# Two-layer attention kernel: the main loop's order on the four compute engines written out by hand, and the first v loads spread over chunks

## The chip, the cores and the metric

The kernel runs on one core of one Trainium2 chip. The metric is device time of one execution in microseconds. It was run three times before the change: 2247.88, 2250.13 and 2253.04 us, median 2250.13 us.

## The reference

For each of two batches, q and k (6080 x 256) are normalised per column, S = kn^T qn / tau is a 256 x 256 matrix, a softmax runs over its last axis, and v (6080 x 256) is multiplied with it. The result x (12160 x 256) goes through two layers with a hidden width of 2048:

```python
h = x @ w_in;  r = np.maximum(h, 0.0);  g = s * (r * r) + b;  x = g @ w_out     # layer 1
h = x @ w2_in; g = h * np.cos(h);       x = g @ w2_out                          # layer 2
```

q and k arrive as float32; the weights arrive as float64 and are turned into float32 on the chip.

## The kernel before

**Numbers.** Every float32 operand is split into a rounded part hi and a remainder lo (`split`, L84: a copy on ScalarE, a subtraction on VectorE or GpSimd), and a product takes three matmuls: hi*hi, hi*lo, lo*hi (`product`, L294).

**Stages.** A prologue (L494 to L578) computes S of batch 0 from 15 chunks of rows; a full chunk has four tiles of 128 rows, 24 matmuls. Chunk loads run three chunks ahead (`qk_load`, QB = 3). In chunk 8 (`c == last - 6`, L546) it also asks for the first two weight blocks (`cv_load`) and for the four v tiles of the first token pair (`x_load`, four DMAs of 64 KB each, in pieces of 128 bytes). Behind the chunks stand the conversion of the first two weight blocks (`cv_conv`), the turning of v (`x_turn`) and its splits, and the softmax (`soft_2`, `soft_3`). The softmax matrix is folded into w_in (`fold`), so that v itself is the input of layer 1.

**Main loop** (L762). The tokens are 12 pairs of two column blocks (512 columns, 480 in every sixth pair); the hidden width is 8 slices. A unit is one pair and one slice, 96 units for each layer, 192 in all. The eight units of the first pair are plain (`in_plain`: 48 matmuls with those of `out`). All later ones use a Winograd product of seven instead of eight block products: with its 24 output matmuls a unit has 21 + 24 = 45. A unit k runs its seven products in four groups, `in_1` and `in_5`, `in_62`, `in_73`, `in_4`, with the outputs of unit k-1 between them (`out`, in the order 0, 1, 3, 2); its element work is `el_a` (relu, or the whole turns of the cosine), `el_b` (square, or sine and product) and `el_c` (split), which straddle units k and k+1. In PSUM there are two banks "s" (`a` and `e` of a unit), one "u" and one "x" (`b` of a unit; "x" alone for side work in layer 1), and four for the outputs "y".

**Around it.** In the units j = 0 to 7 of a pair the next pair's input is made ready: `x_load`, `x_turn` (layer 1), then seven operands (`x_step`: a subtraction for four of them, a split for each). At the first unit of a pair `drain` takes the four finished output blocks of the last pair out of PSUM, to DRAM. Side work is hung on slots of units (`at`): conversion of layer 1's weights (`cv_next`) and their folding in the plain pair, 48 chunks of the batch 1 matrix (`qk1_a`, `qk1_b`) in units 9 to 39, softmax and folding of batch 1 (`soft1`, `fold1`) in units 39 to 48, conversion of layer 2's weights (`cv2_next`, 16 blocks) in units 50 to 93, loads of them (`l2_load`) from unit 89 on.

**What sets the order.** The program is a list, but the instructions' order on each engine is chosen by a planner at build time: it takes what its own cost model holds to be ready, by priority. Slots run at a raised priority (`PW` = 30, L843), drains at `PV` = 40 (L827). SyncE's queue issues all DMAs.

```python
for fn in slot.pop(4 * k_ + s, []):    # L844, under tc.high_priority(offset=PW)
```

Of the kernel before, what the change touches and what calls it, by code (L numbers as in the profile page):

```python
# [28 lines left out]
GB = 8  # L29
# [11 lines left out]
def fused_kernel(ctx: ExitStack, tc: tile.TileContext, q, k, v, tau, w_in, w_out, ms, mb, w2_in, w2_out, res):  # L41
# [49 lines left out]
    def conv(raw, cp, nx=2):  # L91
# [101 lines left out]
    def combine_plain(j):  # L193
# [42 lines left out]
    def x_load(p, t, m):  # L236
# [11 lines left out]
        B[p, m, t] = r  # L248

    def x_turn(p, t, m):  # L250
        if p < NP:
            n = width(p)
            u = st("vturn")
            dve.transpose(out=u[:, 0:n], in_=B.pop((p, m, t))[:, 0:n])
            B[p, m, t] = u

    def x_split(p, nm, src):
        n = width(p)
        if p > NP and nm in ("T3", "T4"):
            hi, lo = [lp[0].tile([P, BLK], F32R, tag="xp", name=f"x{h}", bufs=8) for h in "hl"]  # L260
        else:
            hi, lo = [wk.tile([P, BLK], F32R, tag="xo", name=f"x{h}", bufs=XO) for h in "hl"]
        split(src[:, 0:n], hi[:, 0:n], lo[:, 0:n])
        X[p, nm] = (hi, lo)

    def x_sub(p, a, b):
        n = width(p)
        t = st("xt")
        dve.tensor_tensor(out=t[:, 0:n], in0=a[:, 0:n], in1=b[:, 0:n], op=ALU.subtract)  # L269
        return t  # L270

    def x_step(p, i):

        if i == 0:
            x_split(p, "B11", B[p, 0, 0])
        elif i == 1:
            B[p, "T1"] = x_sub(p, B[p, 0, 1], B[p, 0, 0])
            x_split(p, "T1", B[p, "T1"])
        elif i == 2:
            x_split(p, "B21", B[p, 1, 0])  # L280
        elif i == 3:
            B[p, "T2"] = x_sub(p, B[p, 1, 1], B[p, "T1"])
            x_split(p, "T2", B[p, "T2"])
# [21 lines left out]
    def in_plain(k_, i):  # L305
        f, t = divmod(i, 2)
        nh[0] += 1
        h = sbank() if nh[0] % 3 else bank("u")
# [4 lines left out]
    def in_1(k_):  # L313
        n = at_unit(k_)[3]
        U[k_, "a"] = a = sbank()
        product(a, k_, *IDX[1], True, False)
        l2 = k_ >= NL
        b = bank("x" if l2 and k_ % 2 else "u")
        if NL <= k_ < NL + 2:
            product(b, k_, *IDX[1], True, False)  # L320
        U[k_, "b"] = b

    def in_5(k_):
# [3 lines left out]
    def seed_b(k_):  # L327
# [4 lines left out]
    def copy_5(k_):  # L332
        n = at_unit(k_)[3]
        s5 = wm.tile([P, BLK], F32, tag="s5", name="s5", bufs=1)
        act.copy(out=s5[:, 0:n], in_=U[k_, "e"][:, 0:n])
        U[k_, "s5"] = s5

    def in_62(k_):
        n = at_unit(k_)[3]
        product(U[k_, "b"], k_, *IDX[6], False, False)  # L340
        e = U[k_, "e"]
        dve.tensor_tensor(out=e[:, 0:n], in0=U[k_, "s5"][:, 0:n], in1=U[k_, "b"][:, 0:n], op=ALU.add)  # L342
        product(U[k_, "a"], k_, *IDX[2], False, True)
        U[k_, 0], U[k_, 1] = U.pop((k_, "a")), e

    def in_73(k_):
        n = at_unit(k_)[3]
        product(U[k_, "b"], k_, *IDX[7], False, False)
        product(U.pop((k_, "e")), k_, *IDX[3], False, True)
# [4 lines left out]
    def in_4(k_):  # L354
# [4 lines left out]
    def el_a(k_, i):  # L359
        p, j, l, n = at_unit(k_)  # L360
        h = U[k_, i]
        plain = p == 0
        if l == 0:
            if i == 3 and not plain:
                RR[k_, i] = h
                return
            r = wm.tile([P, BLK], F32, tag="r", name="r", bufs=RB)
            act.activation(out=r[:, 0:n], in_=h[:, 0:n], func=AF.Relu)  # L368
        else:
            q_ = lp[0].tile([P, BLK], I32, tag="n2", name="n2", bufs=2)  # L370
            r = wm.tile([P, BLK], F32, tag="r", name="r", bufs=RB)
            act.activation(out=q_[:, 0:n], in_=h[:, 0:n], func=AF.Copy, bias=0.25)  # L372
            dve.scalar_tensor_tensor(out=r[:, 0:n], in0=q_[:, 0:n], scalar=-1.0, in1=h[:, 0:n], op0=ALU.mult, op1=ALU.add)  # L373
        RR[k_, i] = r

    def el_b(k_, i):
        p, j, l, n = at_unit(k_)
        r, h = RR[k_, i], U.pop((k_, i))
        if l == 0:
            if r is h:  # L380
                dve.scalar_tensor_tensor(out=r[:, 0:n], in0=h[:, 0:n], scalar=0.0, in1=h[:, 0:n], op0=ALU.max, op1=ALU.mult)
            elif i == 2 or p == 0 and i != 1:
                act.activation(out=r[:, 0:n], in_=r[:, 0:n], func=AF.Square)
            else:
                dve.tensor_tensor(out=r[:, 0:n], in0=r[:, 0:n], in1=h[:, 0:n], op=ALU.mult)  # L385
        else:
            act.activation(out=r[:, 0:n], in_=r[:, 0:n], func=AF.Sin, bias=HALF_PI, scale=TWO_PI)  # L387
            dve.tensor_tensor(out=r[:, 0:n], in0=r[:, 0:n], in1=h[:, 0:n], op=ALU.mult)  # L388
# [491 lines left out]
```

## Time and profile before

| | |
|---|---|
| runs | 2247.88, 2250.13, 2253.04 us; median 2250.13 us |
| the profiled execution's own time | 2245.69 us |
| its span, first to last instruction | 2243.9 us |
| instructions | 28456 |
| mean granted TensorE clock | 0.986 |

The profile shows one execution. In its tables PE is TensorE's matmuls, PEld its weight loads, DVE is VectorE, ACT ScalarE, POOL GpSimd, SP SyncE with its DMA queue SPq. An engine's line in a timeline has the start in us, the duration, the line of the kernel, what it writes and reads, and in brackets how long the engine had been idle and who released it. Matmuls are pipelined: a matmul's row lasts 0.39 us, while the next one starts 0.23 us after it, so the distance between starts is the price of one.

### The profile page before, as it was taken

Reading aid. Unit: us, or ns where it says so; the run is one execution under the profiler, and the core shown is the slowest. Engines: PE = TensorE matmul, PEld = TensorE weight load, DVE = VectorE, ACT = ScalarE, POOL = GpSimd, SP = SyncE. Lnnn points to the kernel's source line nnn. Section 1 sums busy time; section 2 is a strip of 40 time slices with the busy share of each in tenths; the row PEclk is TensorE's granted clock in tenths of the full one; section 3 lists DMA queues with packets and bytes.
Section 4 is the critical chain, followed back from the end, with each engine's and each line's share of the span. In section 5 each row is a group of like instructions: output and inputs, shape, how many; then the busy total and the mean of one; then the engine's idle time right before and its main releaser. Section 6 shows DMA issues by size and latency. Waiting matters only on the chain.

```text
span 2243.9 us, 28456 instructions
## 1 busy us (share of the span) xinstructions
PE 2135.6 (95%) x9478; PEld 1733.6 (77%) x9478; DVE 1708.5 (76%) x2412; ACT 1566.6 (70%) x2829; POOL 862.6 (38%) x638
## 2 busy tenths in 40 slices
PE   7799999999989999999999999999999999999998
PEld 7687788787877777788887877777777777777786
DVE  7896777767667988866668688687787787886875
ACT  6686666666666766665657777777777777777775
POOL 0012444334243323322223454444444545444544
PEclk9799999999999999999999999999999999999999
DMA  8531121220213424111042011011011011010111
GB/s 249 143 118 43 34 75 52 57 74 17 66 47 91 131 85 127 36 38 37 21 163 102 9 30 38 1 38 33 6 38 27 11 38 24 15 38 10 23 20 18
DMA packets 255524, 124.81 MB, mean 56 GB/s; under 512 B 206736, under 2 KB 221840, under 8 KB 255376
## 3 DMA queue, kind: packets, MB, share of 16 engines
q1 hardware_dynamic: 255376, 122.99, 20.4%
q8 instruction: 74, 1.21, 0.2%
q14 instruction: 74, 0.61, 0.1%
HBM read 82.31 MB, written 40.63 MB: 55 GB/s over the span
## 4 chain that ended last, share of the span: by engine, by line
PE 46%; DVE 14%; ACT 8%; issue 3%; DMA 1%; DVEq 0%; SPq 0%; POOLq 0%; ACTq 0%; POOL 0%
PE ps_y L408 24%; PE ps_s L299 12%; PE ps_u L299 6%; PE ps_x L299 3%; DVE xt L269 2%; DVE r L388 2%; ACT n L372 2%; ACT gh L85 2%; DVE r L373 2%; ACT r L387 2%; DVE xl L86 2%; DVE gl L86 1%; DVE r L385 1%; DVE ps_s L342 1%; DVE Af L170 1%
## 5 line engine op out<-in xcount | busy, mean ns | idle before, releaser
L86 POOL TENSOR_TENSOR gl<-r,gh 128x512 fp32r<-128x512 f32 (+1 forms) x560 | 747.9, 1342 | 1091.4 <-ACT gh L85 943.9
L85 ACT CAST gh<-r 128x512 fp32r<-128x512 f32 (+1 forms) x680 | 418.3, 615 | 242.5 <-DVE r L385 162.4
L408 PE MATMUL ps_y<-gh,WOh 128*128 128x512 f32 (+1 forms) x1536 | 483.2, 392 | 1.6 <-DVE dr L422 1.2
L408 PE MATMUL ps_y<-gh,WOl 128*128 128x512 f32 (+1 forms) x1536 | 482.9, 391 | 0.0
L408 PE MATMUL ps_y<-gl,WOh 128*128 128x512 f32 (+1 forms) x1536 | 477.9, 389 | 0.4 <-POOL gl L86 0.4
L408 PEld LDWEIGHTS ps_y<-gh,WOh 128*128 128x128 f32 x1536 | 288.6, 189 | 65.3 <-DVE dr L429 2.2
L408 PEld LDWEIGHTS ps_y<-gh,WOl 128*128 128x128 f32 x1536 | 290.0, 189 | 59.5 <-issue 0.2
L408 PEld LDWEIGHTS ps_y<-gl,WOh 128*128 128x128 f32 x1536 | 288.9, 189 | 60.4 <-POOL gl L86 1.2
L387 ACT ACTIVATE r<-r 128x512 f32<-128x512 f32 (+1 forms) x384 | 239.9, 628 | 133.5 <-DVE r L373 133.4
L299 PE MATMUL ps_s<-xh,WIh 128*128 128x512 f32 (+1 forms) x780 | 310.7, 398 | 11.6 <-DVE r L388 8.9
L299 PE MATMUL ps_s<-xh,WIl 128*128 128x512 f32 (+1 forms) x780 | 305.8, 393 | 0.0
L299 PE MATMUL ps_s<-xl,WIh 128*128 128x512 f32 (+1 forms) x780 | 305.4, 391 | 0.0
L299 PE MATMUL ps_u<-xh,WIh 128*128 128x512 f32 (+1 forms) x429 | 173.9, 405 | 32.1 <-DVE ps_s L342 16.8
L299 PEld LDWEIGHTS ps_s<-xh,WIh 128*128 128x128 f32 x780 | 147.5, 189 | 59.3 <-DVE r L388 24.6
L368 ACT ACTIVATE r<-ps_s 128x512 f32<-128x512 f32 (+1 forms) x198 | 116.9, 591 | 92.2 <-PE ps_s L299 91.5
L299 PEld LDWEIGHTS ps_s<-xh,WIl 128*128 128x128 f32 x780 | 147.4, 189 | 31.8
L299 PEld LDWEIGHTS ps_s<-xl,WIh 128*128 128x128 f32 x780 | 147.7, 189 | 28.2
L299 PE MATMUL ps_u<-xl,WIh 128*128 128x512 f32 (+1 forms) x429 | 167.5, 390 | 0.0
L299 PE MATMUL ps_u<-xh,WIl 128*128 128x512 f32 (+1 forms) x429 | 167.3, 390 | 0.0
L373 DVE SCALAR_TENSOR_TENSOR r<-n,ps_s 128x512 f32<-128x512 int32 (+1 forms) x192 | 130.0, 677 | 46.2 <-ACT n L372 45.0
L388 DVE TENSOR_TENSOR r<-r,ps_s 128x512 f32<-128x512 f32 (+1 forms) x192 | 129.4, 674 | 44.4 <-ACT r L387 42.5
L86 DVE TENSOR_TENSOR gl<-d,gh 128x512 fp32r<-128x512 f32 (+1 forms) x88 | 106.2, 1206 | 62.7 <-ACT gh L85 53.3
(160 smaller groups left out, 3417.0 us busy)
## 6 DMA issues: line engine op xcount, KB each, us to landing
xraw<-in_v_dram SPq DMA_DIRECT2D x160, 64.0 KB, 2.5
ys<-dr SPq DMA_DIRECT2D x40, 256.0 KB, 2.3
xraw<-ys SPq DMA_DIRECT2D x40, 256.0 KB, 3.1
out_dram<-dr SPq DMA_DIRECT2D x160, 64.0 KB, 2.0
raw<-in_moe_w_in_dram SPq DMA_DIRECT2D x16, 512.0 KB, 4.0
raw<-in_moe_w_out_dram SPq DMA_DIRECT2D x16, 512.0 KB, 3.8
qk<-in_k_dram SPq DMA_DIRECT2D x47, 128.0 KB, 2.0
qk<-in_q_dram SPq DMA_DIRECT2D x47, 128.0 KB, 2.2
```

Source lines behind the costliest of these rows:

```text
L85: act.copy(out=hi, in_=x)
L86: (eng or dve).tensor_tensor(out=lo, in0=x, in1=hi.bitcast(F32), op=ALU.subtract)
L170: dve.tensor_tensor(out=Af[:, x, :], in0=Af[:, a, :], in1=Af[:, b, :], op=op)
L269: dve.tensor_tensor(out=t[:, 0:n], in0=a[:, 0:n], in1=b[:, 0:n], op=ALU.subtract)
L299: pe.matmul(acc[:, 0:n], lhsT=a[:, w, :], rhs=b[:, 0:n], start=(start and s == 0), stop=(stop and s == 2), skip_group_check=True)
L342: dve.tensor_tensor(out=e[:, 0:n], in0=U[k_, "s5"][:, 0:n], in1=U[k_, "b"][:, 0:n], op=ALU.add)
L368: act.activation(out=r[:, 0:n], in_=h[:, 0:n], func=AF.Relu)
L372: act.activation(out=q_[:, 0:n], in_=h[:, 0:n], func=AF.Copy, bias=0.25)
L373: dve.scalar_tensor_tensor(out=r[:, 0:n], in0=q_[:, 0:n], scalar=-1.0, in1=h[:, 0:n], op0=ALU.mult, op1=ALU.add)
L387: act.activation(out=r[:, 0:n], in_=r[:, 0:n], func=AF.Sin, bias=HALF_PI, scale=TWO_PI)
L388: dve.tensor_tensor(out=r[:, 0:n], in0=r[:, 0:n], in1=h[:, 0:n], op=ALU.mult)
L408: pe.matmul(accs[p, t][m][:, 0:n], lhsT=wo[w][:, f, m * P:(m + 1) * P], rhs=g[x][:, 0:n], start=(j == 0 and f == 0 and s == 0), stop=(j == ...
```

## The change

Helpers become generators that stop after each small step (`yield`), and `steps` hangs one step on each of a list of places (unit, hook). A unit has eight hooks, 0 to 7 (12 in the plain pair). A manual schedule holds TensorE, ScalarE, VectorE and GpSimd to the written order from the main loop on; SyncE's order stays with the planner. High priorities in the loop are gone. The arithmetic is the same. In the prologue the first v tiles are asked for one at a time, in chunks 6 to 9, and the two weight blocks in chunks 5 and 11; the third conversion no longer stands ahead of the loop. The loads of the batch 1 chunks run two ahead instead of one. The 16 conversions of layer 2's weights take one step at hooks 0, 1, 6 and 7 from unit 50 on, 128 steps in all. `soft_1` is merged into `soft1`, with one square root for both norms.

```diff
-            if c == last - 6:
+            if c == last - 9:
                 cv_load()
-                for m_ in range(2):
-                    for t_ in range(2):
-                        x_load(0, t_, m_)
+            if last - 8 <= c < last - 4:
+                x_load(0, c % 2, (c - last + 8) // 2)
+            if c == last - 3:
                 cv_load()
...
+        at(k0, 1 if l2 else 7, lambda p=p: [x_load(p, t, m) for m in range(2) for t in range(2)])
+        if p < NP:
+            for i, pl in enumerate(((1, 0), (1, 7), (2, 0), (2, 7))):
+                at(k0 + pl[0], pl[1], lambda p=p, i=i: x_turn(p, i % 2, i // 2))
+        if l2:
+            for i in range(7):
...
+                    operand(p, i, [(k0 + i + 1, 0), (k0 + i + 1, 7), (k0 + i + 2, 0)])
+        else:
+            for i in range(4):
+                operand(p, i, [(k0 + i + 3, 0), (k0 + i + 3, 4), (k0 + i + 3, 7)])
+            operand(p, 4, [(k0 + 7, 0), (k0 + 7, 1), (k0 + 7, 3)])
+            operand(p, 5, [(k0 + 7, 2), (k0 + 7, 4), (k0 + 7, 7)])
+            operand(p, 6, [(k0 + 8, 0), (k0 + 8, 1), (k0 + 8, 2)])
...
+    ms_ = ctx.enter_context(tc.manual_schedule(engines={mybir.EngineType.PE, mybir.EngineType.Activation, mybir.EngineType.DVE,
+                                                        mybir.EngineType.Pool}))
...
+        if live:
+            mm1(k_)
+            mm5(k_)
+        if old:
+            first(b, 2)
+        if live:
+            seed(k_)
+        if two_b:
+            rest(b, 2)
+        hook(k_, 0)
+        if live:
+            copy5(k_)
+        out(b, 0)
+        if old:
+            g_hi(b, 1)
+            lo(b, 1)
+        hook(k_, 1)
+        if live:
+            mm6(k_)
+        if two_b:
+            sine(b, 2)
+        elif old:
+            sq_act(b, 2)
+        if live:
+            add6(k_)
+            mm2(k_)
+        if two_b:
+            sine(b, 3)
+            mult(b, 2)
+        out(b, 1)
+        hook(k_, 2)
+        if live:
+            first(k_, 0)
+        if old:
+            g_hi(b, 2)
+            lo(b, 2)
+        if two_b:
+            mult(b, 3)
+        if live:
+            mm7(k_)
+        hook(k_, 3)
+        if live:
+            (rest if two else mult)(k_, 0)
+        if old:
+            g_hi(b, 3)
+            lo(b, 3)
+        if live:
+            add7(k_)
+            mm3(k_)
+        if live and two:
+            sine(k_, 0)
+        hook(k_, 4)
+        out(b, 2)
+        if live:
+            first(k_, 1)
+            if two:
+                mult(k_, 0)
+            g_hi(k_, 0)
+            (rest if two else mult)(k_, 1)
+            lo(k_, 0)
+        hook(k_, 5)
+        if edge:
+            drain(p - 1, 0, 0)
+        if live:
+            if two:
+                turns(k_, 3)
+                sine(k_, 1)
+                rest(k_, 3)
             else:
...
+                relu_sq(k_, 3)
+        out(b, 3)
+        if live:
+            mm4(k_)
+        hook(k_, 6)
+        if live and two:
+            mult(k_, 1)
+        if edge:
+            drain(p - 1, 0, 1)
+        hook(k_, 7)
+        if edge:
+            drain(p - 1, 1, 0)
+            drain(p - 1, 1, 1)
```

Here b is unit k-1, `mm1` to `mm7` are the seven products, `first` is relu or `turns`, `rest`, `sine` and `mult` are layer 2's steps of the cosine, `g_hi` and `lo` are the split of a result (GpSimd subtracts for all four results in layer 2, for 0 and 1 in layer 1), `add6` and `add7` are the two additions of the Winograd scheme, which read `b`.

## Rows read from the trace of the kernel before

**Rows 1.** The page: busy time, share of the span and instructions of each engine.

```profile
PE 2135.6 (95%) x9478; PEld 1733.6 (77%) x9478; DVE 1708.5 (76%) x2412; ACT 1566.6 (70%) x2829; POOL 862.6 (38%) x638
```

**Rows 2.** The chain of waits: start us, us, what; two quiet stretches, one broken.

```profile
1023.74 2.72 PE ps_y L408 x12
1033.94 2.72 PE ps_y L408 x12
...
1328.55 2.75 PE ps_y L408 x12
...
1339.05 2.75 PE ps_y L408 x12
...
1571.55 3.35 DVE xt L269 x2
```

**Rows 3.** Pairs 1, 6, 9, 11, 15, 23: length; PE, PEld, DVE, ACT, POOL; clock; DMA.

```profile
201.70:294.50 92.80, 90.61 (x428) 75.11 (x427) 67.31 (x85) 61.20 (x111) 36.10 (x26) 1.00 0.21 55
...
681.10:773.90 92.80, 84.62 (x361) 66.63 (x360) 81.70 (x124) 64.08 (x117) 30.61 (x20) 1.00 0.36 109
...
954.20:1036.30 82.10, 81.89 (x362) 67.49 (x361) 56.33 (x74) 50.17 (x90) 21.36 (x16) 1.00 0.12 26
...
1117.70:1198.00 80.30, 79.64 (x365) 67.89 (x364) 50.91 (x70) 48.84 (x90) 18.69 (x15) 1.00 0.50 167
...
1460.70:1548.80 88.10, 85.78 (x362) 67.88 (x362) 68.63 (x97) 66.22 (x120) 42.98 (x33) 0.98 0.12 25
...
2157.10:2233.90 76.80, 76.03 (x343) 62.99 (x342) 53.98 (x82) 56.35 (x105) 37.92 (x32) 1.00 0.09 15
```

**Rows 4.** SyncE's queue in the prologue, timeline.

```profile
37.15 13.39 SPq L246 DMA_DIRECT2D xraw<-in_v_dram  x16
...
51.17 0.41 SPq L512 DMA_DIRECT2D rk<-in_k_dram  x1
```

**Rows 5.** TensorE's and VectorE's timelines, prologue to first main matmul.

```profile
63.00 1.01 PE L541 MATMUL ps_y<-qkh 128*128 128x384 f32 x2 [10.42 <-ACT qkh L526]
...
85.69 0.80 PE L299 MATMUL ps_s<-xh,WIh 128*128 128x512 f32 x1 [0.66 <-ACT WIh L189]
...
66.28 0.42 DVE L96 TENSOR_SCALAR cx<-raw 128x512 int32<-128x512 int32 x1
...
80.87 0.69 DVE L101 SCALAR_TENSOR_TENSOR cx<-ca,cx 128x512 f32<-128x512 f32 x1
```

**Rows 6.** Windows of the prologue, columns as in rows 3.

```profile
30.00:35.00 5.00, 5.00 (x34) 5.00 (x34) 4.70 (x5) 3.49 (x5) 0.00 (x0) 1.00 0.95 299
...
65.00:70.00 5.00, 5.00 (x21) 5.00 (x21) 4.18 (x10) 1.32 (x3) 0.00 (x0) 0.57 0.01 2
```

**Rows 7.** Timelines of a layer 2 unit: TensorE, ScalarE, VectorE hand work on.

```profile
1589.73 0.39 PE L299 MATMUL ps_s<-xh,WIl 128*128 128x512 f32 x1
...
1590.21 0.60 ACT L372 ACTIVATE n<-ps_s 128x512 int32<-128x512 f32 x1
...
1590.91 0.69 DVE L373 SCALAR_TENSOR_TENSOR r<-n,ps_s 128x512 f32<-128x512 int32 x1 [0.74 <-ACT n L372]
...
1592.30 0.69 DVE L388 TENSOR_TENSOR r<-r,ps_s 128x512 f32<-128x512 f32 x1 [0.70 <-ACT r L387]
1592.90 0.68 DVE L351 TENSOR_TENSOR d<-s,ps_u 128x512 f32<-128x512 f32 x1
```

**Rows 8.** Groups by line (count, busy us, mean ns); a tile's durations (min/median/max).

```profile
L373 DVE SCALAR_TENSOR_TENSOR r<-n,d 128x512 f32<-128x512 int32 (+1 forms) x96 | 100.2, 1044 | 12.7 <-ACT n L372 12.4 <-issue 0.3
...
L269 DVE TENSOR_TENSOR xt<-xraw x24: 614/1682/1786, 1127.9 to 2094.8; 128x512 f32<-128x512 f32 x20, 128x480 f32<-128x480 f32 x4
```

**Rows 9.** SyncE's queue at a pair's edge in layer 1, timeline.

```profile
390.49 0.43 SPq L246 DMA_DIRECT2D xraw<-in_v_dram  x1
...
392.15 8.03 SPq L246 DMA_DIRECT2D xraw<-in_v_dram  x15
```

**Rows 10.** The page: DMA issues, KB each, median us to landing.

```profile
xraw<-in_v_dram SPq DMA_DIRECT2D x160, 64.0 KB, 2.5
```

More of the change, by code (lines that the diff above doesn't have):

```diff
@@ L352, in in_73, with mm4 @@
         U[k_, 3] = d
-    def in_4(k_):
+    def mm4(k_):
         product(U[k_, "b"], k_, *IDX[4], False, True)
         U[k_, 2] = U.pop((k_, "b"))
[L359 to L374, printed above, removed]
@@ new lines, in turns, with rest, sine @@
+    def turns(k_, i):
+        n = at_unit(k_)[3]
+        U[k_, i, "n"] = q_ = lp[0].tile([P, BLK], I32, tag="n2", name="n2", bufs=2)
+        act.activation(out=q_[:, 0:n], in_=U[k_, i][:, 0:n], func=AF.Copy, bias=0.25)
+    def rest(k_, i):
+        n = at_unit(k_)[3]
+        RR[k_, i] = r = r_tile()
+        dve.scalar_tensor_tensor(out=r[:, 0:n], in0=U.pop((k_, i, "n"))[:, 0:n], scalar=-1.0, in1=U[k_, i][:, 0:n],
+                                 op0=ALU.mult, op1=ALU.add)
+    def sine(k_, i):
+        n = at_unit(k_)[3]
+        r = RR[k_, i]
+        act.activation(out=r[:, 0:n], in_=r[:, 0:n], func=AF.Sin, bias=HALF_PI, scale=TWO_PI)
@@ new lines, in at, with hook, steps, run @@
+    def at(k_, h, fn):
+        slot.setdefault((k_, h), []).append(fn)
+    def hook(k_, h):
+        for fn in slot.pop((k_, h), []):
+            fn()
+    def steps(gens, places):
+        gens, places = list(gens), iter(places)
+        def run():
+            while gens:
+                try:
+                    next(gens[0])
+                    return
+                except StopIteration:
+                    gens.pop(0)
+                    return
+        for k_, h in places:
+            at(k_, h, run)
+        return gens
@@ new lines, in fused_kernel, with qk1_place @@
+    steps([lazy(combine_plain, 0)], [(NJ - 1, h) for h in (1, 3, 5, 7, 9, 11)])
+    for j in range(1, NJ):
+        steps([lazy(combine_plain, j)], [(NJ - 1 + j, h) for h in (0, 1, 2, 3, 4, 6)])
+    steps([lazy(colsum)], [(NJ, h) for h in range(4)])
+    at(NJ, 7, qk1_open)
+    places = [(u, h) for u in range(NJ + 1, NU0 - NJ - 1) for h in (0, 2, 4, 6)]
+    active = []
+    def qk1_place(i):
+        for g in list(active):
+            if next(g, 0) == 0:
+                active.remove(g)
+        if i is not None:
+            g = qk1(i)
+            next(g)
+            active.append(g)
@@ new lines, in fused_kernel, with first, lo @@
+    cv_fold()
+    def first(k_, i):
+        if k_ >= NL:
+            turns(k_, i)
+        elif i != 3:
+            relu(k_, i)
+    def lo(k_, i):
+        g_lo(k_, i, pool if k_ >= NL or i < 2 else dve)
+    ms_ = ctx.enter_context(tc.manual_schedule(engines={mybir.EngineType.PE, mybir.EngineType.Activation, mybir.EngineType.DVE,
+                                                        mybir.EngineType.Pool}))
+    for k_ in range(NJ):
+        for i in range(4):
+            in_plain(k_, i)
+            hook(k_, 3 * i)
+            relu(k_, i)
+            if i == 1:
+                mult(k_, i)
+            else:
+                sq_act(k_, i)
+            hook(k_, 3 * i + 1)
+            if k_:
+                out(k_ - 1, i)
+            g_hi(k_, i)
+            hook(k_, 3 * i + 2)
+            g_lo(k_, i, dve)
@@ new lines, in fused_kernel @@
+    for k_ in range(NJ, NU + 1):
+        p, j = divmod(k_, NJ)
+        b = k_ - 1
+        live, old = k_ < NU, b >= NJ
+        two, two_b = k_ >= NL, b >= NL
+        edge = j == 0
+        if two and k_ < NL + NJ:
+            l2_use(j)
+        if live:
[66 more added lines that the diff above has]
+                rest(k_, 3)
+            else:
+                relu_sq(k_, 3)
[11 more added lines that the diff above has]
+            drain(p - 1, 1, 1)
```

451 lines of the change are left out of this document (218 added, 233 removed).

## The prediction

> **What bounds the kernel now.** I read the page first: TensorE is busy 95% of the span, no other engine over 76% [rows 1]. That row can't show how much is waiting, since a matmul's row is longer than its price, so the second view is the chain of waits. In quiet stretches it meets the same output block every 10.20 us (1023.74, 1033.94), in layer 2 every 10.50 (1328.55, 1339.05) [rows 2]: 45 matmuls at 0.227 us, in layer 2 about 0.233, and nothing else. Where the chain breaks, it runs over VectorE (xt, r) for some 10 us: there TensorE waits [rows 2].
>
> The third view prices that by pairs [rows 3]. Pair 9 takes 82.1 us for 360 matmuls; 8 units of 10.2 are 81.6, so it hardly waits. Pair 15 has the same matmuls and takes 88.1: 6.5 over, 2.0 of it the slower pace (8 x 0.25, which I take no order to remove), 4.5 waiting. Pair 6 takes 92.8: 11.2 of waiting, with VectorE busy 82 us. Pair 1 with some 68 narrow matmuls (half as wide, so 0.117 each, 8.0 in all) has 92.8 - 89.6 = 3.2. Done so for all 23 Winograd pairs (one row each, six shown), waiting is 28 us in pairs 1 to 5, 30 in pairs 6 to 11, and pairs 12 to 23, layer 2, are 68 over, of which 24 is pace and 44 waiting. These 102 us, and the prologue, are what an order can win.
>
> The prologue's loss is seen in the queue: SyncE spends 13.39 us on issuing the 16 v loads, and the last chunk loads follow at 51.17 [rows 4]. TensorE stands for 10.42 us until 63.00 [rows 5], and after it the granted clock is 0.57, for most of that window the lower level, 1.2 GHz [rows 6].
>
> **The change, part by part.**
>
> *v loads spread.* Between two chunk loads SyncE now issues four v loads (4 x 0.84 = 3.35 us, [rows 4]) and two chunk loads (0.4 each): 4.1 us, where TensorE takes 3.5 for a chunk's 24 matmuls (34 in 5 us, [rows 6]). Four chunks fall back 0.6 each, 2.4 us, hidden by the three chunks loaded ahead. The 10.4 us gap goes, and 2 us of slow clock. What is late next is VectorE: from 65 to 70 us it is busy 4.18 of 5 [rows 6]; but from 66.28 to 80.87 it also runs conversions of the third to fifth block (0.42 and four steps of 0.69 each, some 3 us, [rows 5]), which now stand in the loop. So the first main matmul comes at 85.7 - 9 = 77. Unit 0 gives 2 back: it has 8 us for TensorE (no outputs yet), but those conversions lie in it and keep VectorE and ScalarE some 10 us. Net **-7** (0 if the conversions only move, -12 if nothing is given back).
>
> *A unit in layer 1*, from the start of mm1 (0.227 a matmul, T = 10.2). The hand-overs are read from rows: last matmul's start to ScalarE 0.48, ScalarE to VectorE or back 0.7 from start to start, back to back on VectorE 0.6 [rows 7]. mm6's last matmul starts at 3.17, so add6 at 3.6; g_hi(b,2) at 4.84, lo(b,2) 5.54 to 6.25 (out(b,2) wants it at 7.7); mult(k,0) to 6.85, lo(b,3) to 8 (wanted at 9.07); add7 to 8.6 (mm4 wants it at 9.52); mult(k,1) to 9.2 (the next mm5 wants its bank at 10.88). Every wait has 0.9 us to spare or more, so a plain run of such units has none. The batch 1 chunks add TensorE 0.7 us each, more than they add to a slack; their loads run two ahead, some 14 us, against at most 8.5 us of v issue [rows 9].
>
> *The turns of v.* Here the change adds a wait. x_load stands at hook 7 of the edge unit, behind the drains to DRAM of the first two blocks, and takes 0.53 us an issue [rows 9]: the first tile is issued about 2 us into the next unit at the latest, lands some 4 us later (3 x 0.53 and 2.5, [rows 10]), and x_turn stands at that unit's hook 0. Before, x_turn stood a whole unit behind x_load. VectorE now stands some 3.5 us with add6, lo(b,2) and mult behind it; add6 ends at 6.7 where mm3 wants it at 6.1 plus the side matmuls. With chunk matmuls in the unit (pairs 1 to 5) that is 0 to 1 us, without them 1.5, and with a conversion step on top (pairs 6 to 9) 2.4.
>
> *Layer 2's weight conversions* take 128 single steps at four hooks a unit, 32 units instead of the crowd of pair 6 [rows 3]. VectorE then has 5.3 us of the unit's own (five steps of 0.6 to 0.7, two SBUF-only ones near 1.04, [rows 7, 8]), 2.35 of conversion (a block 2.5, [rows 5], and some 2.2 for what follows it; 16 in 32 units), up to 2.7 of operands: 10.35 in the worst unit, so it sits at the bound there and 1 to 2 us a pair stay. Together layer 1 keeps 9 of 28 us in pairs 1 to 5 and 21 of 30 in pairs 6 to 11: **-28** (bounds +12, below, and -50, if nothing waits).
>
> *A unit in layer 2* (T = 10.4). VectorE: rest(b,2) at 0.95, an operand's lo and subtraction to 3.6, add6 3.7, mult(b,2) 4.3, mult(b,3) 4.9, rest(k,0) 5.7, add7 6.45, mult(k,0) 7.1 behind sine(k,0), rest(k,1) 7.9, rest(k,3) from 9.0 to 10.1, mult(k,1) to 10.7; mm5 of the next unit wants that bank at 11.06. ScalarE has 14 steps of 0.6 at most, 8.4 us [rows 7]. So it fits with 0.3 us. The spread operands are the risk: xt takes 614 ns at best and 1682 at the median [rows 8]; 1 us more in front of add6 runs through the whole chain and costs some 0.4 in four units of a pair. That leaves 1.5 us a pair (0 to 4), 18 of 44: **-25** (-40 to +5). The edge's four drains cost VectorE 2.5 us where no operand stands; I take them as hidden by that, else 0.7 a pair.
>
> The slow xt rows fall where GpSimd works. The Trainium skill (SBUF — State Buffer, "Who interferes with whom") states that VectorE with two SBUF inputs and GpSimd take a shared port pair as an exclusive lock, for a whole instruction. By that rule every such step of mine could wait for a whole GpSimd step; the trace agrees in the extreme, 1786 against 614 ns, and it is the rival below.
>
> *Rest.* Colsum, softmax of batch 1, fold and l2_load in steps: no price, their waits are covered by the unit around them; without cover 4 us. Tail: the same drains, 0 (+-2).
>
> Sum against the profiled execution's own 2245.69 us (span 2243.9): -7 - 28 - 25 = -60, 2186. The median of the runs is 4.4 above it, so **2190**.
>
> **The rivals.**
> 1. *Clean:* every order wait has its slack, also the turns, as SyncE's order is the planner's and may run ahead: -12 - 50 - 40 = -102, 2148. Against it: the v loads started between the drains' DMAs before, too [rows 9], and not earlier.
> 2. *The turns decide:* each of 11 edges pays the whole wait and turn, 5 us, and 15 stays elsewhere: layer 1 at 70 of waiting, +12. With -7 and -25: 2230.
> 3. *The order is given back:* a strict order makes waits as long as those removed, 2250. For it: the planner's order has no idle TensorE in pairs 9 and 10 either; against it: the 11.2 us of pair 6, which that order made by crowding.
> 4. *Slower, by VectorE in layer 2:* the place is the chain add6 to mult(k,1). r<-n,d averages 1044 ns [rows 8]; if the SBUF-only steps of a unit (two of its own, half a subtraction, 7/8 of a lo) all took xt's 1.7 us, VectorE needs 4.8 + 5.7 + 0.35 of drains + 0.7 for two hand-overs that nothing fills: 11.6 us. 96 x 11.6 = 1114 against 1036 now (1198 to 2234, [rows 3]): +78, less 35 from the rest: 2293. It decides from 11.15 us a unit. For it: the order can't step around a slow instruction any more. Against it: GpSimd is busy 43 of 88 us [rows 3], so about half of these steps run alone.
>
> **How the numbers follow.** My forecast 0.50, clean 0.12, turns 0.15, given back 0.08, slower 0.15. The measurement can tell 0.2% (4.5 us) from no change. Faster: 0.50 + 0.12 + 0.15 + 0.02 = 0.79; same 0.06, slower 0.15. The range reaches from clean to given back, 2145 to 2252; outside lie rival 4 and the far ends of my terms. My forecast's own range is 2160 to 2215.
>
> **What would show it.** Right: the gap before 63 us is gone and the first main matmul comes near 77; pairs 6 and 7 fall to about 86; layer 2's pairs to 84.5 to 85.5, with VectorE's operands one or two to a unit; VectorE waits for a v load at the start of every pair's second unit. Wrong: layer 2 units over 10.6 us with TensorE waiting for mult, or waits of add6 over 2 us in every pair, or a prologue that ends at 85 again.

## The result, and the profile after

The changed kernel takes 2170.73 us (median of four runs, 2168.9 to 2171.85) where the kernel before took 2250.93 us beside it: a ratio of 0.9644, interval 0.9627 to 0.9661. The forecast was 2190 in a range of 2145 to 2252. So it is faster, and by more than the forecast. The profiled span fell from 2243.9 to 2167.1 us, 76.8 less.

The page: TensorE is now busy 97% of the span and ScalarE 73% (70% before); VectorE and GpSimd are within a point of what they were [rows 1].

```profile
PE 2108.6 (97%) x9478; PEld 1734.0 (80%) x9478; DVE 1656.3 (76%) x2410; ACT 1577.3 (73%) x2829; POOL 852.6 (39%) x638
```

The same pairs as in [rows 3] (1, 6, 9, 11, 15, 23), same columns. There and in all that follows pairs and units are cut at TensorE's last output matmul of a unit, which starts some 9.3 us after the unit's first matmul. What is called the first unit of a pair below is therefore mostly the second one in the program, at whose hook 0 the turn of v stands.

```profile
188.30:283.00 94.70, 92.17 (x433) 75.75 (x432) 82.80 (x121) 66.57 (x122) 50.44 (x35) 1.00 0.22 56
655.30:739.50 84.20, 82.41 (x361) 67.35 (x360) 66.60 (x101) 56.77 (x104) 27.48 (x19) 1.00 0.23 66
913.80:1001.60 87.80, 83.76 (x361) 68.53 (x360) 70.76 (x104) 57.33 (x106) 27.14 (x19) 0.98 0.28 81
1089.60:1168.90 79.30, 79.26 (x365) 67.96 (x365) 48.94 (x70) 47.90 (x90) 18.57 (x16) 1.00 0.54 179
1419.50:1502.60 83.10, 83.10 (x361) 66.95 (x360) 65.47 (x96) 67.52 (x119) 41.06 (x33) 1.00 0.12 25
2080.00:2156.60 76.60, 75.72 (x343) 63.41 (x342) 53.00 (x80) 56.43 (x104) 37.91 (x32) 1.00 0.09 15
```

In pair 15 no gap is left between TensorE's rows (83.10 busy of 83.10). Pair 6 is 8.6 us shorter. Pair 9, which hardly waited before, **grew** from 82.1 to 87.8. By stretch, from 2243.9 to 2167.1: start to end of the plain pair -13.4 (201.7 to 188.3), pairs 1 to 11 -15.7 (996.3 to 980.6), pairs 12 to 23 -48.2 (1035.9 to 987.7), tail +0.5.

The prologue: SyncE issues v in four parts between chunk loads [rows 4], and the first main matmul starts at 77.13 (85.69 before [rows 5]).

```profile
31.13 2.33 SPq L249 DMA_DIRECT2D xraw<-in_v_dram  x4
...
36.72 2.53 SPq L249 DMA_DIRECT2D xraw<-in_v_dram  x4
...
41.84 2.75 SPq L249 DMA_DIRECT2D xraw<-in_v_dram  x4
...
47.33 2.24 SPq L249 DMA_DIRECT2D xraw<-in_v_dram  x4
```

```profile
77.13 0.80 PE L294 MATMUL ps_u<-xh,WIh 128*128 128x512 f32 x1 [0.56 <-ACT WIh L189]
```

Layer 2's operand steps (a tile's durations, min/median/max, of xt and xl) are all at one length; before, the median of xt was 1682 ns [rows 8]:

```profile
L281 DVE TENSOR_TENSOR xt<-xraw x24: 649/684/687, 1120.2 to 2052.2; 128x512 f32<-128x512 f32 x20, 128x480 f32<-128x480 f32 x4
...
L274 DVE TENSOR_TENSOR xl<-xraw,xh x36: 651/684/687, 1119.6 to 2051.6; 128x512 fp32r<-128x512 f32 x30, 128x480 fp32r<-128x480 f32 x6
```

The edge into pair 9, which begins at 913.8: SyncE's queue, then VectorE, then TensorE, then two windows.

```profile
913.42 0.32 SPq L436 DMA_DIRECT2D ys<-dr  x1
916.63 0.32 SPq L455 DMA_DIRECT2D kept<-cl  x1
917.04 0.38 SPq L436 DMA_DIRECT2D ys<-dr  x1
917.48 8.95 SPq L249 DMA_DIRECT2D xraw<-in_v_dram  x16
926.53 0.91 SPq L436 DMA_DIRECT2D ys<-dr  x2
927.53 0.40 SPq L736 DMA_DIRECT2D raw<-in_moe_w_in_dram  x1
```

```profile
922.19 0.71 DVE L257 STREAM_TRANSPOSE vturn<-xraw 128x512 f32<-128x512 f32 x1 [3.99 <-DMA xraw<-in_v_dram]
```

```profile
924.14 0.50 PE L294 MATMUL ps_u<-xh,WIh 128*128 128x512 f32 x1 [3.87 <-DVE ps_s L333]
```

```profile
924.00:928.00 4.00, 3.86 (x12) 3.06 (x13) 3.73 (x8) 1.11 (x2) 0.66 (x1) 0.68 0.81 150
928.00:932.00 4.00, 4.00 (x17) 3.25 (x16) 3.65 (x5) 1.65 (x3) 1.16 (x1) 0.90 0.87 285
```

VectorE stands 3.99 us at the turn of v. The v loads leave at 917.48, behind two stores that wait for their data: a converted weight (`kept<-cl`) and an output block. Behind VectorE's wait TensorE idles 3.87 us, and then the granted clock is 0.68 and 0.90, so partly at 1.2 GHz: 0.32 x 4 + 0.10 x 4 = 1.7 us more. Together 5.6 of the 5.8 us by which this unit exceeds its matmuls. In pairs 7 to 10 the first v load leaves 3.7 us after the edge, in pairs 3 to 6 only 0.0 to 0.6. The first units of pairs 2 to 10 exceed theirs by 1.2, 1.0, 1.7, 0.4, 2.1, 3.9, 5.8, 5.8 and 6.6 us: 28.5 in all.

### The profile page after: what moved, and what is told of

Read it like the earlier page. It is cut to its first block, busy times and chain, and to the rows that moved or that the text cites. A ratio compares the mean times of both kernels' runs of the same rounds, so it can differ in the third digit from the quotient of the medians.

```text
span 2167.1 us, 28250 instructions
## 1 busy us (share of the span) xinstructions
PE 2108.6 (97%) x9478; PEld 1734.0 (80%) x9478; DVE 1656.3 (76%) x2410; ACT 1577.3 (73%) x2829; POOL 852.6 (39%) x638
## 4 chain that ended last, share of the span: by engine, by line
PE 79%; DVE 4%; ACT 1%; issue 1%; DMA 1%; SPq 1%; POOL 0%; DVEq 0%; ACTq 0%; POOLq 0%
PE ps_y L419 41%; PE ps_s L294 21%; PE ps_u L294 11%; PE ps_x L294 4%; PE ps_x L659 1%; DMA xraw<-in_v_dram 1%; DVE r L375 1%; PE ps_x L179 1%; SPq L249 0%; DVE gl L406 0%; DVE ps_s L333 0%; DVE cx L97 0%; DVE d L380 0%; ACT r L363 0%; ACT gh L401 0%
## 5 line engine op out<-in xcount | busy, mean ns | idle before, releaser
L406 POOL TENSOR_TENSOR gl<-r,gh 128x512 fp32r<-128x512 f32 (+1 forms) x560 | 728.3, 1308 | 1096.7 <-ACT gh L401 711.2
L419 PE MATMUL ps_y<-gh,WOh 128*128 128x512 f32 (+1 forms) x1536 | 474.7, 390 | 0.2 <-ACT gh L401 0.2
L419 PE MATMUL ps_y<-gl,WOh 128*128 128x512 f32 (+1 forms) x1536 | 472.8, 389 | 0.7 <-POOL gl L406 0.7
L419 PE MATMUL ps_y<-gh,WOl 128*128 128x512 f32 (+1 forms) x1536 | 473.0, 389 | 0.0
L375 DVE TENSOR_TENSOR r<-r,ps_s 128x512 f32<-128x512 f32 (+1 forms) x374 | 251.4, 672 | 5.9 <-ACT r L363 5.3
L333 DVE TENSOR_TENSOR ps_s<-s,ps_u 128x512 f32<-128x512 f32 (+1 forms) x136 | 93.6, 688 | 199.2 <-ACT r L369 59.7
L396 ACT ACTIVATE r<-r 128x512 f32<-128x512 f32 (+1 forms) x384 | 228.9, 621 | 3.7 <-DVE r L390 3.7
L385 ACT ACTIVATE n<-ps_s 128x512 int32<-128x512 f32 (+1 forms) x192 | 114.3, 595 | 84.1 <-PE ps_s L294 84.0
```

The source lines that it names most:

```text
L333: dve.tensor_tensor(out=U[k_, "e"][:, 0:n], in0=U[k_, "s5"][:, 0:n], in1=U[k_, "b"][:, 0:n], op=ALU.add)
L385: act.activation(out=q_[:, 0:n], in_=U[k_, i][:, 0:n], func=AF.Copy, bias=0.25)
L406: eng.tensor_tensor(out=lo[:, 0:n], in0=RR.pop((k_, i))[:, 0:n], in1=hi[:, 0:n].bitcast(F32), op=ALU.subtract)
L419: pe.matmul(accs[p, t][m][:, 0:n], lhsT=wo[w][:, f, m * P:(m + 1) * P], rhs=g[x][:, 0:n], start=(j == 0 and f == 0 and s == 0), stop=(j == ...
```

## The experiments

Every kernel is the changed one with the edit shown. The kernel before ran beside each group: 2246.05 us (first four runs), 2249.39 (next four), 2247.19 and 2247.11 (the last two groups). "Over its matmuls" is a unit's or pair's time less its matmuls at 0.2267 us each (10.2 / 45); narrower ones count by their width.

**The order alone: the planner gets its freedom back.**

```diff
-    ms_ = ctx.enter_context(tc.manual_schedule(engines={...}))
```

> The changed program without the manual schedule: same steps at the same places of the list, but the planner picks each engine's order again (and no raised priorities). Theory: the fixed order itself is the gain in layer 2: its pairs go back to 86 to 88 us, 2215 to 2235 in all. Rival: finer steps and their places are enough for any order: 2165 to 2180.

2230.08 us, ratio 0.9928 (0.9908 to 0.9947). Against the changed kernel's span the loss is 59.3 us: 37.5 in layer 2 (1025.2 against 987.7), 19.8 in pairs 1 to 11, 3.8 in the plain pair, and a gain of 1.7 ahead of it. A layer 2 pair is back at 87.1 (pair 14), as the theory had it:

```profile
1364.00:1451.10 87.10, 84.42 (x361) 67.10 (x360) 68.28 (x96) 65.85 (x119) 43.34 (x33) 1.00 0.12 25
```

So all of the change but the written order (single steps, spread loads, no raised priorities) gave 17.5 of the 76.8 us, 11.3 of it up to the end of the plain pair; the written order gave the rest.

**The v loads of the prologue at once again, in chunk 8.**

```diff
-            if c == last - 9:
+            if c == last - 6:
                 cv_load()
-            if last - 8 <= c < last - 4:
-                x_load(0, c % 2, (c - last + 8) // 2)
-            if c == last - 3:
+                for m_ in range(2):
+                    for t_ in range(2):
+                        x_load(0, t_, m_)
                 cv_load()
```

> The changed kernel with the first v tiles and both weight blocks asked for at once in chunk 8, as before the change. Theory: SyncE's queue makes the gap, so TensorE stands some 10 us before the last chunks again and the first main matmul comes at 84 to 86 instead of 77: 2177 to 2181. Rival: VectorE's work bounds the prologue and the conversions that moved out of it gave the 8 us: first main matmul at 77 to 79, 2170 to 2173.

2182.17 us, ratio 0.9711 (0.9696 to 0.9725). The block holds SyncE 14.59 us, TensorE's gap is back and the first main matmul is 8.1 us later, as the theory had it:

```profile
39.31 14.59 SPq L249 DMA_DIRECT2D xraw<-in_v_dram  x16
```

```profile
65.40 1.01 PE L549 MATMUL ps_y<-qkh 128*128 128x384 f32 x2 [9.83 <-ACT qkh L534]
...
85.24 0.80 PE L294 MATMUL ps_u<-xh,WIh 128*128 128x512 f32 x1 [0.56 <-ACT WIh L189]
```

The span is 13.7 us longer, and the time is just over the theory's range. The rest lies in the first units of pairs 6 to 10, which the edit does not touch: in this execution the granted clock is 0.50 for 4 us behind the waits of pairs 7 to 10, and those units exceed their matmuls by 6.4 to 6.7 us.

**The turns of v a unit later (pairs 2 on).**

```diff
-            for i, pl in enumerate(((1, 0), (1, 7), (2, 0), (2, 7))):
+            for i, pl in enumerate(((1, 0), ...) if first else ((2, 0), (2, 7), (3, 0), (3, 7))):
```

> The changed kernel with the four turns of v one unit later (hooks 0 and 7 of units 2 and 3 of a pair instead of 1 and 2; pair 1's stay). Theory: VectorE's stand at the first turn is what the pairs' first units pay; they lie 28 us over their matmuls in pairs 2 to 10, so 25 us less than the changed kernel's 2170.7: 2143 to 2150, with pairs 9 and 10 back at 82 us. Rival: the edges pay for drains and conversion steps, which VectorE has there in any case: 2165 to 2171, and the wait moves to another step.

2156.14 us, ratio 0.960 (0.9584 to 0.9616). The first units lose their wait (pair 10 falls from 88.0 to 82.0), but the second units of pairs 7, 8 and 9 now exceed their matmuls by 5.1, 5.9 and 2.7 us. Pair 8, SyncE and VectorE:

```profile
825.77 10.26 SPq L249 DMA_DIRECT2D xraw<-in_v_dram  x16
837.20 0.40 SPq L736 DMA_DIRECT2D raw<-in_moe_w_in_dram  x1
```

```profile
842.32 0.43 DVE L97 TENSOR_SCALAR cx<-raw 128x512 int32<-128x512 int32 x1 [6.06 <-DMA raw<-in_moe_w_in_dram]
```

The weight block queues behind the sixteen v issues. Neither number of the record came out: the wait moved down SyncE's queue by one load.

**The v loads of pairs 2 to 11 in the pair before, a tile at a time.**

```diff
+        if 1 < p < NP:
+            for i in range(4):
+                at(k0 - 4 + i, 3, lambda p=p, i=i: x_load(p, i % 2, i // 2))
+        else:
             at(k0, 1 if l2 else 7, ...)
```

> The v loads of pairs 2 to 11 are issued one tile (4 DMAs) at a time in units 4 to 7 of the pair before, and the turns stay where the changed kernel has them. Theory (the first unit of a pair is long because VectorE stands at the turn of v until a tile has landed that SyncE issued only in that same unit; and in the run with later turns the sixteen issues in a row delayed the weight loads): the first units of pairs 2 to 10 lose 26 to 28 of their 28.5 us, no second unit grows, and the time is 2138 to 2148. Rival (SyncE is short of time wherever the issues stand, so that the wait only moves to another load, that of q and k in pairs 1 to 4 or of the weights in pairs 6 to 10): 2150 to 2165.

**2140.63 us**, ratio 0.9515 (0.9498 to 0.9532), the best of all. The span is 2138.6, 28.5 under the changed kernel's. The nine first units lose some 25 us (0.1 to 0.6 stays in each), a little less than the 26 to 28 of the theory, and no second unit grows; the rest came in the units beside them, 1.0 of it in pair 1's first. No turn waits for a v load any more, where nine did in the changed kernel, for 32.0 us in all. Pair 9, without wait and at full clock:

```profile
897.10:979.80 82.70, 82.22 (x362) 67.47 (x361) 71.18 (x104) 57.13 (x106) 27.24 (x19) 1.00 0.29 86
```

**The same loads in one block, only five places sooner.**

```diff
-        at(k0, 1 if l2 else 7, lambda p=p: [x_load(p, t, m) for m in range(2) for t in range(2)])
+        if 1 < p < NP:
+            at(k0, 2, lambda p=p: [x_load(p, t, m) for m in range(2) for t in range(2)])
+        else:
+            at(k0, 1 if l2 else 7, lambda p=p: [x_load(p, t, m) for m in range(2) for t in range(2)])
```

> As the run with the early loads, but all sixteen v loads of pairs 2 to 11 in one block at place 2 of the pair's first unit, five places (some 6 us) sooner than in the changed kernel. It tells apart whether being sooner is enough, or whether the issues have to be taken apart. Theory (a block of sixteen issues keeps SyncE for 9 to 10 us, and the loads behind it, of weights in pairs 6 to 10, are late by as much wherever the block stands): the turns' wait is gone from pairs 2 to 6, but conversion steps in pairs 7 to 10 wait 1 to 6 us for their raw tile: 2146 to 2160. Rival (being sooner is all): within 2 us of the run with single tiles, 2139 to 2143.

2140.55 us, ratio 0.9517 (0.9462 to 0.9573): the rival. No conversion step waits. The block of pair 8, whose first unit begins at 814.5:

```profile
796.32 0.38 SPq L736 DMA_DIRECT2D raw<-in_moe_w_out_dram  x1
796.75 11.22 SPq L249 DMA_DIRECT2D xraw<-in_v_dram  x16
820.63 0.38 SPq L736 DMA_DIRECT2D raw<-in_moe_w_in_dram  x1
```

Five places later, in the changed kernel, it left 3.7 us **after** this pair's edge, here 17.7 us before. For SyncE a place is only a rank among its own issues: here the block ranks ahead of the edge's stores and leaves right behind the weight load before it.

**The softmax's last steps a place later, on top of the early loads.**

```diff
-    steps([lazy(soft1)], [..., (u + 1, 2), (u + 1, 4), (u + 1, 5), (u + 1, 6)])
+    steps([lazy(soft1)], [..., (u + 1, 2), (u + 1, 5), (u + 1, 6), (u + 1, 7)])
```

> As the run with the loads one tile at a time in the pair before, and the last three steps of the softmax of layer 1 (the transposes of its exponentials and what follows) one place later. Theory: the 1.9 us that TensorE waited for the exponentials at the end of pair 4 shrinks to under 0.6, and the time is 1 to 2 us below the run without it. Rival (the wait is only moved into the fold behind it): within 0.5 us of that run or above it.

2140.64 us, the same, so the rival. Pair 4's last unit falls from 2.5 to 1.2 us over its matmuls, pair 5's first rises from 0.3 to 1.4: moved, not removed.

**The conversion of layer 2's weights at all eight places.**

```diff
-                 [(u, h) for u in range(NU0 + 2, NL - 2) for h in (0, 1, 6, 7)][1:])
+                 [(u, h) for u in range(NU0 + 2, NL - 2) for h in range(8)][1:])
```

> The conversion steps of the weights of layer 2 stand at all eight places of a unit instead of four, so that they are done in half as many units. Theory (single steps at places apart are what keeps the pace in pairs 6 to 11: two more steps a unit on VectorE and ScalarE come between the steps that TensorE waits for): the units that hold them grow by 0.5 to 1.5 us each, some 20 units, and the units after them lose little: 2178 to 2200. Rival (any fixed place does): 2164 to 2174.

2179.32 us, ratio 0.9688 (0.9667 to 0.9709). Pairs 6 and 7 grow to 95.2 and 100.3 us:

```profile
654.90:750.10 95.20, 87.61 (x361) 65.63 (x360) 77.75 (x122) 61.98 (x115) 30.21 (x21) 1.00 0.33 101
750.10:850.40 100.30, 89.83 (x361) 66.65 (x360) 82.72 (x134) 65.00 (x121) 30.29 (x21) 0.98 0.39 121
```

That is 11.0 and 14.0 us more, about 1.6 a unit, a little over the theory's 0.5 to 1.5; the time is in its range. Pairs 9 and 10, now without conversion, are short again (82.2, 82.4): the first v load leaves at 935.96, with the edge at 935.9; no store of a weight stands ahead of it.

**All operand steps of a layer 2 pair at one place.**

```diff
-    operand(p, i, [(k0 + i + 1, 0), (k0 + i + 1, 7), (k0 + i + 2, 0)])
+    operand(p, i, [(k0 + 2, 0), (k0 + 2, 0), (k0 + 2, 0)])
```

> The changed kernel with all operand steps of a layer 2 pair at one place, hook 0 of the pair's third unit, instead of one or two to a unit. Theory: a crowd of operand steps on VectorE is what cost layer 2 some 4 us in the third unit of each pair before: about 11 steps of 0.65 us against some 2 us free there, 4 to 6 us for 11 pairs, 2215 to 2235. Rival: the crowd was harmless and only the order of the element steps counts: 2170 to 2178.

2280.16 us, ratio 1.015 (1.013 to 1.0171), slower than before and dearer than either theory had it. One unit a pair exceeds its matmuls by about 10 us, and a pair takes 92 to 94 (pair 14 here):

```profile
1357.70:1450.20 92.50, 84.62 (x361) 67.92 (x360) 66.11 (x96) 67.51 (x119) 41.18 (x33) 0.96 0.11 23
```

TensorE there idles 7.88 us until ScalarE's gh, which stands behind seven x_hi, four of them waiting for VectorE's xt; behind the idle time the granted clock falls (0.96 over the pair), which is part of the 10 us. The theory had counted VectorE's steps alone.

**Layer 2's subtractions at place 3, where GpSimd works.**

```diff
-                    operand(p, i, [(k0 + i + 1, 0), (k0 + i + 1, 7), (k0 + i + 2, 0)])
+                    operand(p, i, [(k0 + i + 1, 3), (k0 + i + 1, 7), (k0 + i + 2, 3)])
```

> In layer 2 the first and the last step of each operand stand at place 3 of a unit, where GpSimd is at work, instead of place 0. Theory (what the fixed order gained in layer 2 is that these VectorE steps no longer run beside GpSimd's): the mean of xt<-xraw goes from about 0.68 us to 1.2 or more, stalls come back in the units, 1 to 4 us a pair, and the time is 2182 to 2215. Rival (the steps may run beside GpSimd as long as they stand in a fixed place; they stretch, but VectorE has room): 2166 to 2175.

2310.2 us, ratio 1.027 (1.0248 to 1.0292), far beyond the theory's 2215. Pairs take 95 us; the four units with an xt exceed their matmuls by 2.3 to 3.9 us each, those with an xl alone by 0.7. The durations of xt, then VectorE and GpSimd in one such unit:

```profile
L281 DVE TENSOR_TENSOR xt<-xraw x24: 677/1773/1778, 1123.8 to 2192.2; 128x512 f32<-128x512 f32 x20, 128x480 f32<-128x480 f32 x4
```

```profile
1478.51 0.68 DVE L274 TENSOR_TENSOR xl<-xraw,xh 128x512 fp32r<-128x512 f32 x1
1479.11 1.77 DVE L281 TENSOR_TENSOR xt<-xraw 128x512 f32<-128x512 f32 x1
```

```profile
1478.78 3.27 POOL L406 TENSOR_TENSOR gl<-r,gh 128x512 fp32r<-128x512 f32 x2 [1.66 <-PE ps_y L419]
```

Units at 2.3 and at 3.9 have the same wait of TensorE, 1.9 us for a product of VectorE's. What differs is the granted clock; in pair 15, a unit of either kind:

```profile
1505.90:1518.40 12.50, 10.57 (x46) 8.32 (x45) 8.52 (x13) 9.68 (x19) 5.86 (x5) 1.00 0.03 12
1529.30:1543.40 14.10, 12.17 (x46) 9.49 (x45) 9.17 (x13) 8.22 (x16) 5.84 (x4) 0.88 0.08 31
```

0.12 x 14.1 is 1.7 us, about the 1.6 between them. In the rest two causes lie on each other, the longer step and the new place. Three more runs take them apart.

**GpSimd made busy beside the unmoved step.** Four quarter-tile subtractions, released by xl:

```diff
+        def fill():
+            n, t = width(p) // 4, lp[0].tile([P, BLK // 4], F32, tag="scr", ...)
+            for a in range(4):
+                hi, lo = ...
+                pool.tensor_tensor(out=t[:, 0:n], in0=lo, in1=hi, op=ALU.subtract)
...
+        if p > NP and i in (0, 2, 4, 5) and places[2][1] == 0:
+            at(*places[2], fill)
```

> The places of the changed kernel stay. In layer 2, GpSimd gets four extra subtractions of a quarter tile each (into a scratch tile that nothing reads) exactly where VectorE forms the next operand, in the four of seven units that form one by subtraction, some 44 times in all. It tells the two halves of the 140 us apart that the run with the operands under GpSimd lost. Theory (beside GpSimd the step stretches from 0.68 to 1.2 to 1.8 us, but at place 0 VectorE idles about 1.5 us afterwards, so the stretch is covered; what cost the time was the place, ahead of work that TensorE waits for): xt<-xraw at 1.2 us or more and the time 2168 to 2182. Rival (the stretch costs wherever it is): stalls of 1 to 3 us in four units of each of eleven pairs, 2215 to 2300. If xt<-xraw stays near 0.68, the two engines don't get in each other's way here, and something else stretched it.

2220.68 us, ratio 0.9874 (0.9816 to 0.9931), but it tells something else: xt kept its 684 ns (median), since the extra work starts 0.2 us after it. What cost 4.3 us a pair is GpSimd itself, whose next gl came late (in pairs 13 to 22 TensorE waits 40 times for gl, 35.1 us in all, and never in the changed kernel):

```profile
1449.39 2.41 POOL L873 TENSOR_TENSOR scr<-xl,xh 128x128 f32<-128x128 f32 x4 [2.98 <-DVE xl L274]
1451.76 4.23 POOL L406 TENSOR_TENSOR gl<-r,gh 128x512 fp32r<-128x512 f32 x3
```

```profile
1453.09 0.73 PE L419 MATMUL ps_y<-gl,WOh 128*128 128x512 f32 x2 [0.86 <-POOL gl L406]
```

**The same, sooner.** The four pieces wait only for a value that is ready ahead of place 0, in pairs 13 to 22:

```diff
+            last = NREF[0][:, 0:8].bitcast(F32)
+            pool.tensor_tensor(out=t[:, 0:8], in0=last, in1=last, op=ALU.subtract)
+            for a in range(4):
+                x, hi = ...
+                pool.tensor_tensor(out=t[:, 0:n], in0=x, in1=hi, op=ALU.subtract)
```

> As the run with extra GpSimd work beside the operand steps, in pairs 13 to 22, but the extra work starts sooner (it waits for a value that is ready just ahead of place 0), so that it lies over xl and xt and ends about when the next gl may begin. Nothing of VectorE's is moved. Theory (two engines that both read two SBUF operands slow each other down): xt<-xraw at 1.0 to 1.8 us. As VectorE idles 0.9 to 1.5 us right behind it, the time is 2170 to 2195, most of it from gl starting a little late. Rival (no slowing down; only the order of VectorE's steps mattered): xt<-xraw stays within 0.65 to 0.72 us, and the time is 2168 to 2185.

2182.31 us, ratio 0.9716 (0.9688 to 0.9744). xt is longer without having moved, xl is not:

```profile
L281 DVE TENSOR_TENSOR xt<-xraw x24: 681/949/956, 1121.6 to 2064.5; 128x512 f32<-128x512 f32 x20, 128x480 f32<-128x480 f32 x4
...
L274 DVE TENSOR_TENSOR xl<-xraw,xh x36: 651/684/699, 1121.0 to 2063.9; 128x512 fp32r<-128x512 f32 x30, 128x480 fp32r<-128x480 f32 x6
```

The stretch, 0.27 us, is less than forecast. It hardly shows on TensorE: these units are 0.3 us longer than in the changed kernel (0.5 over their matmuls instead of 0.2), and of TensorE's 31 waits in pairs 13 to 22 29 are for gl.

**The subtraction at place 6 of the unit before.** GpSimd idles there, but a product of VectorE's comes next.

```diff
-                    operand(p, i, [(k0 + i + 1, 0), (k0 + i + 1, 7), (k0 + i + 2, 0)])
+                    operand(p, i, [(k0 + i, 6), (k0 + i + 1, 7), (k0 + i + 2, 0)])
```

> In layer 2 the subtraction that forms an operand stands at place 6 of the unit before instead of place 0, ahead of a product of VectorE's and while GpSimd idles (1451.0 to 1454.4 in the unit shown). Theory (what costs is to be beside GpSimd or ahead of a step that is due; place 6 is neither): xt<-xraw at 0.66 to 0.72 us and 2166 to 2176. Rival (place 0 is the only one with room, every other costs): stalls of 0.7 us or more in four units of each of eleven pairs, 2200 or more.

2197.71 us, ratio 0.9785 (0.9756 to 0.9813): nearer the rival, just short of its numbers (0.7 us and 2200). xt has 678 ns, and still four units of each pair pay 0.6 us more (0.8 over their matmuls instead of 0.2), 44 x 0.6 = 26 of the 28.4 us lost. TensorE waits for the product behind xt:

```profile
1527.38 0.50 PE L294 MATMUL ps_s<-xh,WIh 128*128 128x512 f32 x1 [0.33 <-DVE r L375]
```

So of the 2.3 us at place 3, 0.2 was there before, and 0.5 is the place of xl, which stands there in its plain 684 ns and brings the units that hold it alone from 0.2 to 0.7. The longer xt is 1.1, and some 0.6 is the place of xt, if it costs there what it does at place 6. That is the whole; the units at 3.9 pay the clock besides.

## Why the prediction was right, and where its terms were off

*Bound.* TensorE's waits were the stock to win from; in quiet stretches its matmuls set the time. Both held: a layer 2 pair is at 83.1 us for 81.6 us of matmuls.

*The sum.* Part of its fit is luck. Its errors lie against each other: the first part gave 6 us more than forecast, layer 1 12 less, layer 2 23 more. Of the signs named, the gap before 63 us is gone (no wait of TensorE above 0.85 us is left there), pairs 6 and 7 are at 84.2 and 86.3, and VectorE waits for a v load at the edge of pairs 2 to 10; layer 2's pairs, at 83, are below the 84.5 to 85.5.

*v loads spread: -7, measured -13.4.* The main matmul at 77 was right (77.13), though the 9 us for it were set rather than added up, and the cause is shown by the run with the block of v. Unit 0 gave back 3 where 2 was forecast: 5.3 over its matmuls against 2.3 before. So far that is -5.6. The mis-sized part is the other seven units of the plain pair, -7.8, which the term priced at nothing. Before, TensorE had waited 3.41 us there for the copy of the column sums, and the granted clock behind it was 0.50, then 0.65, for 4 us each, some 3.4 us more:

```profile
181.54 1.09 PE L599 MATMUL ps_x<-ones,row 1*128 1x2 f32 x6 [3.41 <-ACT row L595]
```

```profile
182.00:186.00 4.00, 4.00 (x12) 3.15 (x12) 3.96 (x9) 1.96 (x5) 0.00 (x0) 0.50 0.00 0
```

Both are gone with the single steps. I had put colsum under "Rest" without a price.

*Layer 1: -28, measured -15.7.* The steps hold, two sizes don't. The conversion in single steps was to leave some 10 us in pairs 6 to 10, from VectorE at its bound; 2.3 is left outside the first units (and the dense version shows what the spacing is worth). The turns of v were to cost 11.1 us there (four times 2.4, once 1.5) and cost 24.2. The wait was forecast as 3.5 us and was 3.99 in pair 9, 3.6 on the mean of the nine; what I had wrong is what TensorE makes of it: it had no work left for all of it (3.87 idle), and in pairs 8 to 10 the unit pays 2 to 3 us beyond that, with a granted clock of 0.57, 0.68 and 0.50 in the 4 us behind the wait. The place of the loads was read from [rows 9] rightly, but as a fixed start "behind the drains"; it is a queue position, and two edits that raise it take the whole wait away. In pairs 1 to 5 16.4 us stay instead of 9, of it 2.5 in the unit that waits for the softmax's transposes; TensorE also waits 1.8 us for batch 1 operands (three times), which I had as covered.

*Layer 2: -25, measured -48.2.* Two steps failed. The slow xt did not come: the written order puts operands into GpSimd's pauses, xt takes 684 ns at the median and 687 at most, and so the 18 us of leftover waits were not there. And the slower pace, which I took no order to remove, was partly waiting: of the 68 us over the matmuls some 20 stay in all (pace and end), where I had 24 + 18. The planner run shows it too: its quiet layer 2 units are at 0.1 over their matmuls, where those before had 0.2 to 0.3.

*Rivals.* The clean one is what the early loads reach, beyond what I gave it: 2140.6. The turns were a real cost, 28.5 of the 55 us (11 edges at 5) of that rival. The slower one, VectorE in layer 2 beside GpSimd, did not come about here, but its mechanism is shown: the same order with the xt and xl steps moved to place 3 is at 2310.

What decides is who starts first. In the run at place 3 xl starts 0.27 us ahead of GpSimd's gl and keeps 0.68 us, while xt starts behind it and takes 1.77. In the kernel before, a like xl that starts behind takes as long:

```profile
1210.05 1.79 DVE L86 TENSOR_TENSOR xl<-xt,xh 128x512 fp32r<-128x512 f32 x1
```

```profile
1209.72 1.57 POOL L86 TENSOR_TENSOR gl<-r,gh 128x512 fp32r<-128x512 f32 x1 [3.26 <-ACT gh L85]
```

Of layer 2's xl and xt together, those that start while a whole-tile step of GpSimd is running take 1.71 to 1.79 us at place 3 (44 of them), and those that start before it at most 0.69 (77). In the run with quarter pieces most xl meet the last 0.12 us of a piece and keep 684 ns, xt meets the last 0.40 us and takes 950; the one xl that meets 0.38 us takes 926. The Trainium skill (SBUF — State Buffer, "Who interferes with whom") states that a VectorE instruction with two SBUF inputs contends with a GpSimd instruction that reads SBUF, over a shared port pair that is an exclusive lock. The rows agree, for xt as for xl.

*Left open.* What the last 0.1 to 0.2 us of a layer 2 unit are was not tried, nor were the merged softmax, the batch 1 loads two ahead and the priorities, each alone. That the clock's fall comes from the wait rests on rows alone: with the wait away pair 9 stays at 1.00.

## What to carry to other kernels

With an order written by hand, ask of every step not only how long it is but what stands right behind it: 0.67 us of VectorE was free at one place, cost 0.6 a unit at another, and some 1.6 behind a busy GpSimd, more where the clock fell as well. A DMA queue has an order too, and a place in the program fixes only the rank there: put loads ahead of stores that wait for their data, and look at what queues behind a block of small issues. When a wait is removed, read the next unit for the load that was behind it.

## What was not expected of the hardware

In the changed kernel waits of nearly the same length had different prices. At pair 9's edge 3.87 us were followed by a granted clock of 0.68 and 0.90 and cost 5.6; at pair 7's edge 3.63 us left the clock at 1.00, and the unit exceeds its matmuls by 3.9. Pair 7, TensorE and the two windows behind its wait:

```profile
749.64 0.50 PE L294 MATMUL ps_u<-xh,WIh 128*128 128x512 f32 x1 [3.63 <-DVE ps_s L333]
```

```profile
749.00:753.00 4.00, 3.36 (x15) 2.79 (x16) 3.95 (x7) 1.10 (x2) 0.38 (x1) 1.00 0.58 90
753.00:757.00 4.00, 4.00 (x19) 3.33 (x18) 3.92 (x5) 1.93 (x4) 1.47 (x1) 1.00 0.92 241
```

The length alone does not sort them. Pair 10's wait, 3.53 us, is the shorter one, and the clock behind it was 0.50, the lower level (1.2 GHz) for the whole of 4 us:

```profile
1011.66 0.80 PE L294 MATMUL ps_u<-xh,WIh 128*128 128x512 f32 x1 [3.53 <-DVE ps_s L333]
```

```profile
1011.70:1015.70 4.00, 4.00 (x10) 3.13 (x11) 2.72 (x5) 1.01 (x2) 0.00 (x0) 0.50 0.80 149
```

In the run with the operand steps at place 3, too, waits of one length (1.9 us) left the clock at 1.00 in one unit and at 0.88 in another.

Sixteen issues of 64 KB in pieces of 128 bytes held SyncE's queue for 8.95 us (pair 9) to 14.59 us (the block in the prologue). GpSimd's extra 2.41 us for four quarter tiles delayed TensorE in the units that held them, though GpSimd was busy only 43% of that run.
